# Linear attention and a gated feed-forward layer on one core: the two block transposes of the middle chunks write their 32-word rows side by side, and the plan's numbers are replaced

## The chip, the cores and the metric

The kernel runs on one core of one Trainium2 chip. The time is device time in microseconds (us). Three runs of the kernel before gave 252.01, 252.36 and 253.9 us; the median, 252.36 us, is the time before. A separate execution was taken by the hardware profiler, and all rows shown here come from it.

About 2.5 us either way (1% of the time) is what a measurement of this kernel can tell from no change.

## What is computed

The reference, cut to what matters: a linear attention with products of two 8-wide projections as features, and behind it a feed-forward layer whose gate is a clipped linear function.

```python
batch, n_heads, seq, head_dim, r = 4, 4, 1088, 32, 8
def phi(x):                                   # 64 features per head
    a = einsum('rd,bhsd->bhsr', S1, x)
    b = einsum('rd,bhsd->bhsr', S2, x)
    return einsum('bhsi,bhsj->bhsij', a, b).reshape(..., 64)
kv  = einsum('bhsf,bhsd->bhfd', phi(k), v)
z   = phi(k).sum(axis=2)
x   = einsum('bhsf,bhfd->bhsd', phi(q), kv) / (phi(q) . z + 1e-6)
x   = x.transpose(0, 2, 1, 3).reshape(4352, 128)
h   = x @ w_in                                # 128 x 2048, double precision given
g   = h * clip(h + 3, 0, 6) / 6
out = g @ w_out                               # 2048 x 128
```

## The kernel before

**Chunks.** The 4352 rows are cut into nine chunks of columns (the data lie transposed, a row of x is a column): chunks 0 to 7 have 512 columns, two of each batch, and chunk 8 has the last 64 rows of all four batches, 256 columns. For each chunk the attention gives x (128 x 512), and the feed-forward layer goes over it in eight steps of 256 hidden units.

**A step of the feed-forward layer** (`step`, from L748). x and the weights are split into a high and a low part in a faster float format, so each product is three matmuls: TensorE (PE) makes h (L763, L764, L769, six matmuls for two halves), ScalarE (ACT) makes r = relu(h+3) (L776), VectorE (DVE) makes g = min(r,6)*h (L780), ACT makes the high part gh (L784), GpSimd (POOL) or DVE makes the low part gl = g - gh (L788), and PE adds the products with w_out into o (L807, L808 from gh, L810 from gl). There are two buffers for h, three each for r and g, four each for gh and gl.

**The attention of the keys** (`keys`): PE projects (abps), ACT copies to ab, DVE or POOL multiplies the features ph_k (L458), PE adds up kvps, and the sums of the features over the rows (`total`, L556 to L561) are made by POOL or DVE for batches 1 to 3. ACT copies the result to kvb (L573).

**The attention of the queries.** Chunks 0 and 1 (`queries`) turn their features with PE (phps, L666; copied to phT by ACT, L672), and x again with PE (xps). Chunks 2 to 8 (`far_queries`) turn them with DVE's transpose of 32 x 32 blocks and a trip through device memory: DVE turns ph into pht (L701; L698 for chunk 8), four DMAs write phd (L707), one reads phT (L712), PE makes numerator and denominator (nd, L594), DVE divides (L601 to L605), and for chunks 2 to 7 DVE turns x into xt (L729), four DMAs write xd (L734), one reads xT (L738), ACT makes the high part xh (L635) and DVE or POOL the low part xl (L639). Chunks 2 to 7 are called the middle chunks here. In both of their transposes the result's words are spread out, so that the columns come out in order: neighbouring words of a turned row are written n/2/4 = 64 words apart in L701 and 4 words apart in L729.

**What sets the order.** Every operation is put into a plan with a cost per engine, a due time and the buffers that it needs; `Plan.order` runs a model of the engines over it, takes what is ready in the order of the due times and so fixes the order of instructions on each engine (and for operations marked `dual` whether DVE or POOL does them). The due times come from a table of numbers at the head of the file (L78 to L91): STEP is the planned distance of two steps, LAG the distance from a step's h to its o, LEADS the lead of each attention operation ahead of its chunk's first step. The weights are unpacked from double precision by nine operations per block (L333 to L358, on ACT and DVE), eight blocks in all, during the first 70 us.

The host puts the two parts of the result together (L881 to L883).

Of the kernel before, what the change touches and what calls it, by code (L numbers as in the profile page):

```python
# [80 lines left out]
W_DUE = (23.69, 5.0, 25.05, 37.01, 36.68, 4.34, 28.58, 37.15)
CONV_LEAD = (5.93, -5.53, -0.33, -14.76, 3.75, 22.58, 29.21, 1.33, 1.88)
LOAD_DUE = {'kT_0': -99, 'v_3': -98, 'wiraw0': -97, 'kT_1': -96, 'kT_3': -95, 'qT_1': -94, 'v_0': -93, 'qT_0': -92, 'v_1': -91, 'woraw0': -90, 'v_2': -89, 'kT_2': -88, 'wiraw1': -87}
LEADS = ({'ab': 20.35, 'cp': 18.54, 'ph': 0.97, 'kv': 7.82, 'kvb': 4.29, 'tr': -9.03, 'trcp': 19.03, 'nd': 3.27, 'norm': 21.13, 'xt': 2.41, 'xh': -30.73, 'xl': 17.21, 'k0': 8.88, 'kld': 18.13, 'vld': 11.2, 'qld': -6.47, 'rd': 32.35, 'xw': -22.53, 'xr': -34.19, 'sum': 7.33}, {'ab': 24.06, 'cp': 49.8, 'ph': 14.57, 'kv': 15.67, 'kvb': 12.77, 'tr': -1.26, 'trcp': 2.1, 'nd': 16.83, 'norm': 25.0, 'xt': 46.75, 'xh': 14.66, 'xl': 29.1, 'k0': 3.17, 'kld': 7.72, 'vld': 57.89, 'qld': 71.23, 'rd': 44.5, 'xw': -12.53, 'xr': 8.33, 'sum': -2.02})


HOLD = 5.62
HOLD_DUE = -28.65
SOON = 0.71
SOON_DUE = 11.09  # L90
PATIENCE = 0  # L91

# [193 lines left out]
def fused_kernel(ctx: ExitStack, tc: tile.TileContext, qT, kT, v1, sb, w_in, w_out, outT):  # L286
    nc = tc.nc
# [295 lines left out]
    def divided(c, due, T, t, m, ready, phTb, nb, xb, LEAD, near=True):

# [4 lines left out]
        def nd(_):  # L589
            W["nd"] = bank(nb.tag, f"nd_{c}_{t}")  # L590
            for u, p, e in product(range(m), range(2), (0, HP)):
                o = (2 * u + p) * 2 * DV
# [1 line left out]
                nc.tensor.matmul(W["nd"][e : e + HP, o : o + 2 * DV], T["phT"][:, p, i : i + HP], kvb[batch_of(c0 + i)][:, p, :], start=True, stop=True)  # L594
# [85 lines left out]
    def far_queries(c, due, psb, ndb, ph_eng):  # L680

        LEAD = LEADS[1]
        c0, n = CHUNKS[c]
# [7 lines left out]
        def turn(_):  # L693

            T["turn"] = buf("raw", [P, 4, CH // 2], f"pht_{c}")[:, :, : n // 2]
            src = T["ph"][:, :nt, :].rearrange("p t (e f w) -> p f (t e) w", e=2, w=Q)
            if mixed:
                nc.vector.transpose(T["turn"].rearrange("p f (b w) -> p f b w", w=Q), src)  # L698
# [2 lines left out]
            nc.vector.transpose(out, src.rearrange("p f b (k t) -> p f b k t", t=nt))  # L701

# [22 lines left out]
        def xturn(_):  # L725

            T["xturn"] = buf("xturn", [P, H, nt * Q], f"xt_{c}")
            out = T["xturn"].rearrange("p f (w t) -> p t f w", t=nt)
            nc.vector.transpose(out, T["x"].rearrange("p t (f w) -> p t f w", w=Q))  # L729
# [154 lines left out]
```

## Time and profile before

| | us |
|---|---|
| three runs | 252.01, 252.36, 253.9 |
| the profiled execution, whole | 251.5 |
| its span, first to last instruction | 249.7 |
| transposes pht of chunks 2 to 7 (L701), six | 12.5 |
| transposes xt (L729), six | 6.7 |
| POOL's share of the gl (L788), 41 | 96.6 |
| DVE's share of the gl (L788), 31 | 43.8 |

In the profile a row of the timeline gives start, duration, engine, line, operation, result<-operands, shapes and a count; brackets at its end give the time that the engine stood idle ahead of it and what ended that. PEld is the loading of weights, SPq the queue that issues the DMAs. A matmul's duration covers the filling of its pipeline: matmuls of 512 columns start 0.233 us apart when PE is full (at 104.38, 104.61, 104.84 us and so on), though each is shown with 0.39 us.

### The profile page before, as it was taken

Reading aid. Unit: us, or ns where it says so; the run is one execution under the profiler, and the core shown is the slowest. Engines: PE = TensorE matmul, PEld = TensorE weight load, DVE = VectorE, ACT = ScalarE, POOL = GpSimd, SP = SyncE. Lnnn points to the kernel's source line nnn. Section 1 sums busy time; section 2 is a strip of 40 time slices with the busy share of each in tenths; the row PEclk is TensorE's granted clock in tenths of the full one; section 3 lists DMA queues with packets and bytes.
Section 4 is the critical chain, followed back from the end, with each engine's and each line's share of the span. In section 5 each row is a group of like instructions: output and inputs, shape, how many; then the busy total and the mean of one; then the engine's idle time right before and its main releaser. Section 6 shows DMA issues by size and latency. Waiting matters only on the chain.

```text
span 249.7 us, 4708 instructions
## 1 busy us (share of the span) xinstructions
PE 236.0 (95%) x1816; PEld 183.2 (73%) x1816; DVE 206.8 (83%) x260; ACT 166.5 (67%) x206; POOL 142.5 (57%) x90
## 2 busy tenths in 40 slices
PE   8868999899999899899999998999999999999994
PEld 6656677687677667687887775787878787878894
DVE  1769999999999998786986898988989886467762
ACT  2455698777577666577675765666767776786681
POOL 2515999989589874005835794308750673655302
PEclk9999999999999999999999999999999999999999
DMA  6998833050057156030250313212422130010010
GB/s 209 353 302 306 282 114 84 0 149 23 11 148 190 43 149 204 4 85 0 67 164 3 82 46 86 87 22 62 126 87 43 41 112 18 0 42 0 3 43 21
DMA packets 18006, 23.77 MB, mean 95 GB/s; under 512 B 1728, under 2 KB 11072, under 8 KB 17984
## 3 DMA queue, kind: packets, MB, share of 16 engines
q1 hardware_dynamic: 17984, 23.48, 30.9%
q8 instruction: 14, 0.23, 0.4%
q14 instruction: 8, 0.07, 0.1%
HBM read 16.26 MB, written 7.21 MB: 94 GB/s over the span
## 4 chain that ended last, share of the span: by engine, by line
PE 69%; POOL 11%; DVE 6%; DMA 5%; issue 3%; ACT 2%; SPq 1%; DVEq 0%; ACTq 0%; POOLq 0%
PE o L810 11%; PE o L807 11%; PE o L808 10%; PE h L763 10%; PE h L769 10%; PE h L764 10%; POOL gl L788 7%; PE nd L594 3%; DVE g L780 2%; DMA kT<-kT_dram 2%; POOL ph_q L458 2%; PE abps_k L436 2%; POOL ph_k L458 2%; DMA xT<-xd 1%; DMA xd<-xt 1%
## 5 line engine op out<-in xcount | busy, mean ns | idle before, releaser
L788 POOL TENSOR_TENSOR gl<-g,gh 128x1024 fp32r<-128x1024 f32 (+1 forms) x41 | 96.6, 2360 | 83.9 <-PE o L810 42.3
L776 ACT ACTIVATE r<-h 128x1024 f32<-128x1024 f32 (+1 forms) x72 | 70.4, 979 | 36.6 <-PE h L769 35.0
L780 DVE SCALAR_TENSOR_TENSOR g<-r,h 128x1024 f32<-128x1024 f32 (+1 forms) x72 | 82.2, 1153 | 14.2 <-ACT r L776 8.3
L784 ACT CAST gh<-g 128x1024 fp32r<-128x1024 f32 (+1 forms) x72 | 72.1, 1001 | 21.1 <-PE o L808 13.0
L763 PE MATMUL h<-xh,wi_hi 128*128 128x512 f32 (+1 forms) x144 | 56.5, 392 | 2.8 <-DVE g L780 1.7
L807 PE MATMUL o<-gh,wo_hi 128*128 128x512 f32 (+1 forms) x144 | 55.9, 391 | 0.0
L769 PE MATMUL h<-xl,wi_hi 128*128 128x512 f32 (+1 forms) x144 | 55.0, 383 | 0.0
L764 PE MATMUL h<-xh,wi_lo 128*128 128x512 f32 (+1 forms) x144 | 55.0, 382 | 0.0
L808 PE MATMUL o<-gh,wo_lo 128*128 128x512 f32 (+1 forms) x144 | 54.6, 382 | 0.0
L788 DVE TENSOR_TENSOR gl<-g,gh 128x1024 fp32r<-128x1024 f32 (+1 forms) x31 | 43.8, 1418 | 10.0 <-ACT gh L784 6.0
L810 PE MATMUL o<-gl,wo_hi 128*128 128x512 f32 (+1 forms) x144 | 43.9, 387 | 1.7 <-POOL gl L788 1.7
L763 PEld LDWEIGHTS h<-xh,wi_hi 128*128 128x128 f32 x144 | 27.0, 187 | 10.7 <-PE o L808 1.4
L807 PEld LDWEIGHTS o<-gh,wo_hi 128*128 128x128 f32 x144 | 27.0, 188 | 7.0 <-ACT mag_wo L333 0.4
L810 PEld LDWEIGHTS o<-gl,wo_hi 128*128 128x128 f32 x144 | 25.7, 187 | 8.3 <-POOL gl L788 3.0
L769 PEld LDWEIGHTS h<-xl,wi_hi 128*128 128x128 f32 x144 | 27.0, 188 | 5.8
L808 PEld LDWEIGHTS o<-gh,wo_lo 128*128 128x128 f32 x144 | 27.0, 188 | 5.2
L764 PEld LDWEIGHTS h<-xh,wi_lo 128*128 128x128 f32 x144 | 27.0, 188 | 5.2
L458 POOL TENSOR_TENSOR ph_k<-ab_k 128x512 f32<-128x512 f32 (+1 forms) x9 | 9.1, 1022 | 16.5 <-ACT ab_k L445 16.5
L458 POOL TENSOR_TENSOR ph_q<-ab_q 128x512 f32<-128x512 f32 x14 | 18.2, 1311 | 0.4 <-ACT ab_q L445 0.3
L594 PEld LDWEIGHTS nd<-kvb,phT 128*64 128x64 f32 x272 | 9.1, 137 | 5.1 <-issue 3.0
L701 DVE STREAM_TRANSPOSE pht<-ph_q 128x1024 f32<-128x1024 f32 x6 | 12.5, 2083 | 0.0
L594 PE MATMUL nd<-kvb,phT 128*64 128x66 f32 x272 | 10.9, 226 | 1.1 <-DMA phT<-phd 0.8
(82 smaller groups left out, 185.6 us busy)
## 6 DMA issues: line engine op xcount, KB each, us to landing
phd<-pht SPq DMA_DIRECT2D x24, 128.0 KB, 2.3
phT<-phd SPq DMA_DIRECT2D x6, 512.0 KB, 3.6
wiraw<-w_in_dram SPq DMA_DIRECT2D x4, 512.0 KB, 5.3
qT<-qT_dram SPq DMA_DIRECT2D x8, 256.0 KB, 6.1
woraw<-w_out_dram SPq DMA_DIRECT2D x4, 512.0 KB, 5.1
outT_dram<-os SPq DMA_DIRECT2D x8, 256.0 KB, 2.1
xd<-xt SPq DMA_DIRECT2D x24, 64.0 KB, 1.8
xT<-xd SPq DMA_DIRECT2D x6, 256.0 KB, 2.6
```

The costliest lines, as they stand in the source:

```text
L458: engines[e].tensor_tensor(out, a_, b_, op=ALU.mult)
L594: nc.tensor.matmul(W["nd"][e : e + HP, o : o + 2 * DV], T["phT"][:, p, i : i + HP], kvb[batch_of(c0 + i)][:, p, :], start=True, stop=True)
L763: nc.tensor.matmul(T["h"][:, u, :n], wi_hi[:, f], x, start=True, stop=False)
L764: nc.tensor.matmul(T["h"][:, u, :n], wi_lo[:, f], x, start=False, stop=False)
L769: nc.tensor.matmul(T["h"][:, u, :n], wi_hi[:, f], x, start=False, stop=True)
L776: nc.scalar.activation(T["r"][:, :, :n], T["h"][:, :, :n], AF.Relu, bias=3.0, scale=1.0)
L780: nc.vector.scalar_tensor_tensor(T["g"][:, :, :n], T["r"][:, :, :n], 6.0, T["h"][:, :, :n], op0=ALU.min, op1=ALU.mult)
L784: nc.scalar.copy(T["gh"][:, :, :n], T["g"][:, :, :n])
L788: engines[e].tensor_tensor(T["gl"][:, :, :n], T["g"][:, :, :n], T["gh"][:, :, :n].bitcast(F32), op=ALU.subtract)
L807: nc.tensor.matmul(o, wo_hi[:, f], T["gh"][:, u, :n], start=fp == 0 and u == 0, stop=False)
L808: nc.tensor.matmul(o, wo_lo[:, f], T["gh"][:, u, :n], start=False, stop=False)
L810: nc.tensor.matmul(o, wo_hi[:, f], T["gl"][:, u, :n], start=False, stop=fp == NPAIR - 1 and u == 1)
```

## The change

Both transposes of the middle chunks take the blocks in the order in which they lie in the source and write each block's 32-word rows as neighbouring words. The columns of a middle chunk then come out in another order (four strips of 128 columns are interleaved), which nothing on the chip depends on; the host puts them back. The parameter that told the divisions where the columns lie (`near`) is gone. All numbers of the plan's table are others (of them a line or two is shown), LAG is now a time instead of a multiple of STEP, and some costs in the plan are.

```diff
-LAG = 11.64
+LAG = 25.41
...
-                sums.append(plan.add({POOL: 1.3 * k, DVE: 0.6 * k}, d - LEAD["sum"], [*o3, *sums], total, [phb, sumb], dual=True))
+                sums.append(plan.add({POOL: 1.42 * k, DVE: 0.62 * k}, d - LEAD["sum"], [*o3, *sums], total, [phb, sumb], dual=True))
...
-        kv_done[b] = [plan.add({ACT: 0.23}, due - LEAD["kvb"], [prev], halves, [kvbuf])]
+        kv_done[b] = [plan.add({ACT: 0.43}, due - LEAD["kvb"], [prev], halves, [kvbuf])]
...
-                i = (t + u) * P + e if near else e // HP * n // 2 + (t + u) * HP
+                i = (t + u) * P + e
...
-            src = T["ph"][:, :nt, :].rearrange("p t (e f w) -> p f (t e) w", e=2, w=Q)
-            if mixed:
-                nc.vector.transpose(T["turn"].rearrange("p f (b w) -> p f b w", w=Q), src)
-                return
-            out = T["turn"].rearrange("p f (t b k) -> p f b k t", t=nt, k=Q // nt)
-            nc.vector.transpose(out, src.rearrange("p f b (k t) -> p f b k t", t=nt))
+            src = T["ph"][:, :nt, :].rearrange("p t (e f w) -> p (t e) f w", e=2, w=Q)
+            nc.vector.transpose(T["turn"].rearrange("p f (b w) -> p b f w", w=Q), src)
...
-        a = plan.add({DVE: 0.09 + 0.267 * nt}, due - LEAD["tr"], sorted(set(o3), key=o3.index), turn, [phb, turnb])
+        a = plan.add({DVE: 0.09 + 0.27 * nt}, due - LEAD["tr"], sorted(set(o3), key=o3.index), turn, [phb, turnb])
...
-            out = T["xturn"].rearrange("p f (w t) -> p t f w", t=nt)
+            out = T["xturn"].rearrange("p f (t w) -> p t f w", t=nt)
             nc.vector.transpose(out, T["x"].rearrange("p t (f w) -> p t f w", w=Q))
...
-        a = plan.add({DVE: 0.09 + 0.135 * nt}, due - LEAD["xt"], norms, xturn, [xb, xturnb])
+        a = plan.add({DVE: 0.09 + 0.145 * nt}, due - LEAD["xt"], norms, xturn, [xb, xturnb])
...
-        late = due + LAG * STEP
+        late = due + LAG
...
-    both = {POOL: 0.45, DVE: 0.267}
+    both = {POOL: 0.48, DVE: 0.267}
...
+    far = out[NEAR * CH : B * WHOLE].reshape(-1, P // Q, CH // P, Q, DM).swapaxes(1, 2).reshape(-1, DM)
+    out = np.concatenate([out[: NEAR * CH], far, out[B * WHOLE :]], axis=0)
```

With other numbers in the table the whole order is another. Three places of it. (Behind the line number stand the operation, result<-operands with the buffer's number, and the shape; the lines of the kernel after are 3 lower from the steps on.)

ACT, in the start, where the first batch's kvb is copied. Before:

```order
L445 COPY ab_q_281<-abps_q_258 128x256
L445 COPY ab_q_326<-abps_q_313 128x256
L573 COPY kvb_144<-kvps_272 64x2x33 x2
L333 ACTIVATE mag_wo_384<-woraw_311 128x512
L672 COPY phT_400<-phps_0_374 128x2x2x128
L672 COPY phT_403<-phps_2_386 128x2x2x128
L672 COPY phT_403<-phps_0_393 128x2x2x128
```

After:

```order
L445 COPY ab_k_273<-abps_k_254 128x320
L672 COPY phT_281<-phps_0_268 128x2x2x128
L672 COPY phT_281<-phps_2_276 128x2x2x128
L333 ACTIVATE mag_wi_352<-wiraw_266 128x512
L573 COPY kvb_144<-kvps_286 64x2x33 x2
L445 COPY ab_q_397<-abps_q_374 128x256
```

Two copies of phT and the weight operation (mag) stood behind the copy of kvb and stand ahead of it now.

POOL and DVE, at the sums of the features of batch 2's keys (both halves of the batch: L556, then L558 to L561). Before, on POOL:

```order
L458 TENSOR_TENSOR ph_q_1134<-ab_q_1107 128x512 x2
L556 TENSOR_TENSOR sum_1170<-ph_k_1041 128x512
L788 TENSOR_TENSOR gl_0_1188<-g_0_1138,gh_0_1167 128x1024
L788 TENSOR_TENSOR gl_1_1217<-g_1_1156,gh_1_1186 128x1024
L558 TENSOR_TENSOR sum_1170<-sum_1170,ph_k_1191 128x512
L559 TENSOR_TENSOR sum_1170<-sum_1170,ph_k_1191 128x512
L560 TENSOR_TENSOR sum_1170<-sum_1170,ph_k_1191 128x256
L561 TENSOR_TENSOR sum_1170<-sum_1170 128x256
L788 TENSOR_TENSOR gl_4_1346<-g_4_1287,gh_4_1309 128x1024
```

After, on DVE:

```order
L777 SCALAR_TENSOR_TENSOR g_7_1108<-r_7_1077,h_7_1061 128x1024
L458 TENSOR_TENSOR ph_k_1121<-abps_k_1087,ab_k_1106 128x512 x2
L458 TENSOR_TENSOR ph_k_1121<-abps_k_1087,ab_k_1106 128x256
L558 TENSOR_TENSOR sum_1079<-sum_1079,ph_k_1121 128x512
L559 TENSOR_TENSOR sum_1079<-sum_1079,ph_k_1121 128x512
L560 TENSOR_TENSOR sum_1079<-sum_1079,ph_k_1121 128x256
L561 TENSOR_TENSOR sum_1079<-sum_1079 128x256
L601 TENSOR_SCALAR den_0_1158<-nd_0_1140 128x8
L603 RECIPROCAL rden_0_1160<-den_0_1158 128x8
L605 TENSOR_TENSOR x_1157<-nd_0_1140,rden_0_1160 128x256
L777 SCALAR_TENSOR_TENSOR g_0_1181<-r_0_1165,h_0_1126 128x1024
```

The last four of the five sums went from POOL to DVE, ahead of a division and of the g of chunk 2's first step. The same happens in another place for batch 3's keys, ahead of the g of chunk 4's first step. In all POOL now makes 52 of the 72 gl (41 before), DVE 20 (31 before).

PE, where the low part of one of the two steps 4 of the first two chunks is used (chunks 0 and 1 take turns step by step, so each step stands there twice). Before:

```order
L807 MATMUL o_734<-gh_4_934,wo_hi 128x512
L808 MATMUL o_734<-gh_4_934,wo_lo 128x512
L810 MATMUL o_734<-gl_4_949,wo_hi 128x512 x2
L594 MATMUL nd_2_968<-kvb_146,phT_877 64x66 x8
L763 MATMUL h_6_977<-xh_586,wi_hi 128x512
```

After, just ahead of the same use:

```order
L761 MATMUL h_7_978<-xh_551,wi_lo 128x512
L766 MATMUL h_7_978<-xl_552,wi_hi 128x512
L807 MATMUL o_716<-gl_5_910,wo_hi 128x512 x2
L436 MATMUL abps_k_1004<-s_sb,kT_639 64x64 x8
L804 MATMUL o_774<-gh_4_937,wo_hi 128x512
L805 MATMUL o_774<-gh_4_937,wo_lo 128x512
```

Before, the first h of steps 6 and 7 stand behind the use of gl 4; now they and a projection of keys stand ahead of it (the use itself, of gl_4_947, follows on the four matmuls of gh 4 whose first two are shown), so that more of PE's work lies there between a step's h and the use of its gl.

More of the change, by code (lines that the diff above doesn't have):

```diff
@@ L74 @@
 SPLIT = 2
-STEP = 4.24
-DUES = (-3.53, -2.66, 8.36, 29.13)
-LAG = 11.64
[L81 to L91, printed above, removed]
+STEP = 3.88
+DUES = (-97.17, 16.69, 144.97, 26.48)
+LAG = 25.41
+W_DUE = (213.34, 129.51, -53.04, 57.02, 42.36, 69.04, -12.12, 87.77)
+CONV_LEAD = (-7.3, -110.25, 110.52, -232.21, 32.19, 34.25, 284.17, 95.91, 110.18)
+LOAD_DUE = {'kT_0': -99.0, 'v_3': -88.0, 'wiraw0': -92.0, 'kT_1': -95.0, 'kT_3': -87.0, 'qT_1': -91.0, 'v_0': -94.0, 'qT_0': -97.0, 'v_1': -93.0, 'woraw0': -90.0, 'v_2': -96.0, 'kT_2': -89.0, 'wiraw1': -98.0}
+LEADS = ({'ab': 65.79, 'cp': 87.59, 'ph': -38.82, 'kv': 13.4, 'kvb': 66.99, 'tr': -19.53, 'trcp': -65.04, 'nd': -110.46, 'norm': 130.94, 'xt': 75.73, 'xh': -35.2, 'xl': -82.38, 'k0': -206.76, 'kld': 22.63, 'vld': -5.18, 'qld': -38.58, 'rd': 7.49, 'xw': -123.69, 'xr': -108.27, 'sum': 160.61}, {'ab': 56.41, 'cp': 175.14, 'ph': -71.08, 'kv': 15.48, 'kvb': 8.65, 'tr': 2.52, 'trcp': 40.97, 'nd': 14.31, 'norm': 23.48, 'xt': 1.7, 'xh': -18.86, 'xl': 62.54, 'k0': 13.49, 'kld': -16.71, 'vld': 107.4, 'qld': 67.05, 'rd': 116.53, 'xw': -60.56, 'xr': 105.92, 'sum': 123.01})
+HOLD = 0.11
+HOLD_DUE = 67.05
+SOON = 1.81
+SOON_DUE = 35.22
+PATIENCE = 0.0
 @dataclass(eq=False)
@@ L578, in keys, with divided @@
             prev = plan.add({PE: 0.5}, due - LEAD["kvb"] - 0.5, [a, *sums], turn, [kvbuf, kvTb, sumb], 400)
-        kv_done[b] = [plan.add({ACT: 0.23}, due - LEAD["kvb"], [prev], halves, [kvbuf])]
+        kv_done[b] = [plan.add({ACT: 0.43}, due - LEAD["kvb"], [prev], halves, [kvbuf])]
     x_t, x_ops, x_buf = {}, {}, {}
-    def divided(c, due, T, t, m, ready, phTb, nb, xb, LEAD, near=True):
+    def divided(c, due, T, t, m, ready, phTb, nb, xb, LEAD):
         W = {}
@@ L608, in divided @@
         a = plan.add({PE: 0.03 + 0.3 * m}, due - LEAD["nd"] - lag, [ready, *(o for b in batches for o in kv_done[b])], nd, [phTb, nb, xb], 528 * m)
-        return plan.add({DVE: 0.55 + 0.1 * m}, due - LEAD["norm"] - lag, [a], norm, [nb, xb])
+        return plan.add({DVE: 0.56 + 0.1 * m}, due - LEAD["norm"] - lag, [a], norm, [nb, xb])
     def turn_x(c, due, T, norms, xb, xpb, LEAD):
@@ L718, in far_queries @@
         for t in range(0, nt, 2):
-            norms.append(divided(c, due, T, t, min(2, nt - t), rdop, phTb, Buf(ndb), xb, LEAD, mixed))
+            norms.append(divided(c, due, T, t, min(2, nt - t), rdop, phTb, Buf(ndb), xb, LEAD))
         if mixed:
```

## The prediction

> **What bounds the kernel now.** I read the page first, its busy times and its chain of waits, then the busy times by stage, then PE's timeline for the places where it stands idle.
>
> ```profile
> span 249.7 us, 4708 instructions
> PE 236.0 (95%) x1816; PEld 183.2 (73%) x1816; DVE 206.8 (83%) x260; ACT 166.5 (67%) x206; POOL 142.5 (57%) x90
> PE 69%; POOL 11%; DVE 6%; DMA 5%; issue 3%; ACT 2%; SPq 1%; DVEq 0%; ACTq 0%; POOLq 0%
> ```
>
> PE is busy for 236.0 of 249.7 us and makes 69% of the chain. The change takes nothing from PE's own work, so all that can be won is PE's idle time, 13.7 us, and the time in the start in which it does little. The busy times by stage (bounds; length; PE, PEld, DVE, ACT, POOL; clock; DMA) tell where that idle time lies:
>
> ```profile
> 0.00:24.00 24.00, 19.17 (x389) 15.01 (x389) 15.27 (x38) 10.28 (x21) 8.48 (x18) 1.00 0.89 302
> 24.00:35.00 11.00, 10.38 (x118) 7.15 (x113) 11.00 (x18) 8.02 (x14) 10.54 (x10) 1.00 0.66 228
> 35.00:102.00 67.00, 63.01 (x442) 46.87 (x442) 64.20 (x83) 47.79 (x57) 53.28 (x29) 1.00 0.34 93
> 102.00:200.00 98.00, 96.99 (x622) 75.13 (x619) 85.43 (x90) 67.25 (x75) 48.37 (x26) 1.00 0.23 64
> 200.00:250.00 50.00, 46.47 (x261) 39.01 (x259) 30.87 (x35) 33.14 (x42) 21.88 (x10) 0.99 0.09 30
> ```
>
> In the start PE lacks 4.8 us and is filled up with dummy matmuls besides. From 24 us on DVE is full (11.00 of 11.00, then 64.20 of 67.00), and PE lacks 0.6 and 4.0 us; from 102 to 200 us PE lacks only 1.0 us, and what is left lies in the tail. The waits of PE between 35 and 200 us, from its timeline:
>
> ```profile
> 44.29 0.50 PE L810 MATMUL o<-gl,wo_hi 128*128 128x512 f32 x1 [0.79 <-POOL gl L788]
> 47.69 0.50 PE L810 MATMUL o<-gl,wo_hi 128*128 128x512 f32 x1 [0.33 <-POOL gl L788]
> 63.38 0.50 PE L810 MATMUL o<-gl,wo_hi 128*128 128x512 f32 x1 [0.54 <-POOL gl L788]
> 82.02 0.40 PE L594 MATMUL nd<-kvb,phT 128*64 128x66 f32 x6 [0.77 <-DMA phT<-phd]
> 88.83 0.50 PE L763 MATMUL h<-xh,wi_hi 128*128 128x512 f32 x1 [0.45 <-DVE g L780]
> 101.13 0.50 PE L763 MATMUL h<-xh,wi_hi 128*128 128x512 f32 x1 [1.10 <-ACT xh L635]
> 153.44 0.47 PE L763 MATMUL h<-xh,wi_hi 128*128 128x512 f32 x1 [1.01 <-DVE g L780]
> ```
>
> They add up to 4.99 us, all that PE lacks there. Three are on POOL's gl, two on a g that DVE made late, two on an attention trip through memory that ended late.
>
> **The transposes.** By line, with shapes kept apart (count; busy, mean ns):
>
> ```profile
> L701 DVE STREAM_TRANSPOSE pht<-ph_q 128x1024 f32<-128x1024 f32 x6 | 12.5, 2083 | 0.0
> L729 DVE STREAM_TRANSPOSE xt<-x 128x512 f32<-128x512 f32 x6 | 6.7, 1110 | 0.1
> L698 DVE STREAM_TRANSPOSE pht<-ph_q 128x512 f32<-128x512 f32 x1 | 0.7, 699 | 0.0
> ```
>
> L698, chunk 8's, already writes neighbouring words and takes 699 ns for 512 elements where L729 takes 1110. So xt should fall to 0.70, 0.41 less. For pht with twice the elements 2 x 0.70 = 1.40 is the most; L701 and L729 give (2083 - 1110)/512 = 1.90 ns an element and a fixed part of 0.14, and with that part L698 gives 0.70 + 0.56 = 1.26. I take 1.26, 0.82 less. In all 6 x 0.82 + 6 x 0.41 = 7.4 us of DVE's time. [...]
>
> What of the 7.4 us lies on the path? DVE's rows ahead of the late ones:
>
> ```profile
> 85.66 2.07 DVE L701 STREAM_TRANSPOSE pht<-ph_q 128x1024 f32<-128x1024 f32 x1
> 87.57 1.21 DVE L780 SCALAR_TENSOR_TENSOR g<-r,h 128x1024 f32<-128x1024 f32 x1
> 90.59 1.11 DVE L729 STREAM_TRANSPOSE xt<-x 128x512 f32<-128x512 f32 x1
> 100.46 0.62 ACT L635 CAST xh<-xT 128x512 fp32r<-128x512 f32 x1 [2.03 <-DMA xT<-xd]
> 150.17 2.07 DVE L701 STREAM_TRANSPOSE pht<-ph_q 128x1024 f32<-128x1024 f32 x1
> 152.08 1.21 DVE L780 SCALAR_TENSOR_TENSOR g<-r,h 128x1024 f32<-128x1024 f32 x1
> ```
>
> The g at 87.57, for which PE waits 0.45, stands behind a pht: gone. The xt at 90.59 stands behind the same pht and starts the trip that ends in xh at 100.46, for which PE waits 1.10: 0.82 + 0.41 = 1.23 covers it. The g at 152.08 stands behind a pht: 0.82 of the 1.01. That is 0.45 + 1.10 + 0.82 = -2.4 us. All other transposes lie beside PE's work and are worth nothing by themselves. Bounds: 0, if the order moves these places, and -3.6, if in the stage where DVE is full all its pht and xt count (three and two: 3 x 0.82 + 2 x 0.41 = 3.3) with some of 153.44. A loss I exclude: L698 shows the new form. The wait of 0.77 at 82.02 is for a read of phT behind an earlier pht; the order now has that chunk's transposes ahead by several steps: -0.7 (0 to -0.8).
>
> **The start.** What holds it, from PE, ACT and DVE:
>
> ```profile
> 14.89 0.58 PE L493 MATMUL kvps<-v,ph_k 128*32 128x33 f32 x28 [1.85 <-issue]
> 15.54 0.43 ACT L573 COPY kvb<-kvps 64x66 f32<-64x66 f32 x2 [3.08 <-PE kvps L493]
> 16.00 0.68 ACT L333 ACTIVATE mag_wo<-woraw 128x512 f32<-128x512 f32 x1
> 16.70 1.56 ACT L672 COPY phT<-phps 128x512 f32<-128x512 f32 x3
> 18.08 0.17 DVE L601 TENSOR_SCALAR den<-nd 128x8 f32<-128x8 f32 x1 [2.08 <-PE nd L594]
> ```
>
> DVE stands idle for 2.08 us until the first nd comes, and from there on is full for 50 us; an earlier first nd moves that whole stage. Before, nd had to wait behind kvb (to 15.97), mag (0.68) and the first copy of phT (to about 17.3). Now those copies are done ahead of kvb, and nd can follow it at once: 1.3 us. Besides, the last tile of v that kvps needs is the seventh load of the queue behind the projection's constants instead of the ninth, 2.3 MB down the queue instead of 2.9; at the 302 GB/s of that stage 0.6 MB are 2.0 us. Against that, PE's halt of 1.85 us in kvps is ended by nothing the profile shows and may recur, and the loads ahead of that tile now hold a block of w_in with first place. I take -2.0 (1.3 and a third of the rest; bounds +1.0, half of the 2.0 turned round, and -3.3). Until the first nd DVE's work is about the same.
>
> **The waits for POOL.** The order now lets POOL make more gl (52 x 2.4 us), but gives most of them more time: the use of gl 4 that waited at 63.38 had 6.1 us of matmuls (by 0.233 us each) between its h and itself, and has 13.3 now. Only the first four uses have as little as before (5.4 to 9.3 us; 7.4 to 8.8 before), and it was two of the first five that waited 0.79 and 0.33. I take -1.3 of the 1.66 (bounds 0 and -1.7). Each wait that goes also saves PE's restart (0.50 us in five of the rows above, 0.39 for a matmul in the stream): some five of them, -0.5 (0 to -0.7).
>
> **The sums on DVE.**
>
> ```profile
> L559 POOL TENSOR_TENSOR sum<-sum,ph_k 128x512 f32<-128x512 f32 x3 | 4.8, 1588 | 0.2
> L556 DVE TENSOR_TENSOR sum<-ph_k 128x512 f32<-128x512 f32 x1 | 1.3, 1332 | 0.0
> L458 DVE TENSOR_TENSOR ph_k<-abps_k,ab_k 128x512 f32<-128x512 f32 x8 | 5.2, 685 | 3.0 <-ACT ab_k L445 2.9
> L788 DVE TENSOR_TENSOR gl<-g,gh x31: 692/1226/2710, 77.1 to 244.8; 128x1024 fp32r<-128x1024 f32 x25, 128x512 fp32r<-128x512 f32 x6
> ```
>
> Twice, two additions of 512 and two of 256 go to DVE ahead of a g. The one sum that DVE made took 1.33 us, a product of the same size 0.69; so 1.5 x 0.69 x 2 = 2.1 to 1.5 x 1.33 x 2 = 4.0 us each. The g behind them frees one of two h buffers; PE has another step's h and o to do meanwhile, so I charge half a microsecond each: +1.0 (0 to +8.0, both in full; nearer the low end, because the order puts 3 us and more of o ahead of those h).
>
> **The shorter lag.** The x of chunks 4 and 6 is now asked for late: from the start of nd to the first h that needs xh PE has 11.3 us of work (chunk 4, from its second nd) and 11.2 (chunk 6, from its first). What it took before, from nd on PE to xh:
>
> ```profile
> 134.64 1.16 PE L594 MATMUL nd<-kvb,phT 128*64 128x66 f32 x32
> 146.14 0.61 ACT L635 CAST xh<-xT 128x512 fp32r<-128x512 f32 x1
> 85.63 0.57 PE L594 MATMUL nd<-kvb,phT 128*64 128x66 f32 x12
> 161.62 0.57 PE L594 MATMUL nd<-kvb,phT 128*64 128x66 f32 x12
> 174.12 0.62 ACT L635 CAST xh<-xT 128x512 fp32r<-128x512 f32 x1
> ```
>
> The first pair, 11.5, and 0.6 for xh, less 0.41 for the faster xt, is 11.7: 0.5 late in chunk 6. Behind these places the o of chunk 4's first steps come 5.7 us of matmuls behind their h (20 before): r, g and gh alone need 3.3 us and three hand-overs there, so that nothing is spare. +0.6 (0 to +4.3).
>
> **The sum.** -2.4 - 0.7 - 2.0 - 1.3 - 0.5 + 1.0 + 0.6 = -5.3. The profiled execution took 251.5 us with what lies around its span; that is 0.5 under the lowest of the three runs and 0.9 under their median. 251.5 - 5.3 = 246.2, and 0.5 on it for the runs: 246.7 us.
>
> **The rivals.** *The start and the full stage give all* (chance 0.13): -3.3 in the start, -3.6, -0.8, -1.7, -0.7 and nothing given back: -10.1, 241.9 us. For it: DVE is nearly full from 24 to 102 us, so that each microsecond taken from it there can count. Against: PE has only 4.6 us idle from 24 to 102 us.
>
> *POOL and DVE hold each other up* (0.09): gl on DVE takes 1.23 us at the median and 2.71 at most, so an addition that meets POOL's waits up to 1.5 us. POOL now has 52 gl of 2.4 us and DVE two groups of four sums; if each group waits for one whole gl of POOL, with PE waiting for the g behind, it is 2 x 2.4 more: 251.5, no change. Against: fewer gl on DVE (20) to meet anything. [...]
>
> *The new write pattern is no faster* (0.05), because what slows L701 is something other than its writes: -2.4 and half of the start's gain fall away, 250.1.
>
> *The x of the later chunks comes too late* (0.10; the other side). The trip took 14.83 us once, from 85.63 to 100.46, with other transfers in SP's queue between. With that in chunks 2, 4 and 6, where PE has 12.5, 11.3 and 11.2 us, PE would wait 0.6 + 14.8 - 0.4 less these: 2.5 + 3.7 + 3.8 = 10.0; 246.7 - 0.6 + 10.0 = 256.1. It decides from 8.8 us in all, a trip of some 14.4 us in each of the three. Against it: the longest of the others took 12.5 (161.62 to 174.12).
>
> **How the numbers follow.** The forecast, 244.0 to 249.5 by its own terms, has 0.56; no change for other reasons has 0.07. The range leaves out most of the first rival, the last, and a little beyond: 242.8 to 251.4. A change over 1% is over 2.5 us, about what a measurement of this kernel can tell from none. Faster by that: the forecast and the first rival, 0.69; within it 0.21 (the middle rivals 0.14, the rest 0.07); slower 0.10.
>
> **What would show it.** In the profile after: pht at 1.2 to 1.4 us and xt at 0.7; the first nd less than 0.3 us behind kvb, and before 17; no wait of PE for POOL's gl over 0.3 us behind the first four; PE's waits from 24 to 200 us under 3 us in all; the sums on DVE under 1 us each for 512. I am wrong if pht stays at 2 us, if the first h comes later than 24.05 us as before, or if PE waits for xh or g by over 2 us at the first steps of chunks 2, 4 or 6.

## The result, and the profile after

The changed kernel is slower: 256.39 us (median of 4 runs, 256.27 to 256.64) against 252.44 us for the kernel before (252.01 to 253.9). The ratio is 1.0148, 95% interval 1.0106 to 1.0189. The profiled execution took 256.46 us with a span of 254.7 us; that of before had 249.7. So 5.0 us of span were lost where 5.3 were to be won.

The head of the page after, with the clock's row of the 40 slices:

```profile
span 254.7 us, 4691 instructions
PE 241.4 (95%) x1817; PEld 185.2 (73%) x1817; DVE 189.6 (74%) x251; ACT 165.0 (65%) x206; POOL 163.4 (64%) x99
PEclk9979999999999889999999999999999999999999
PE 83%; DVE 6%; DMA 4%; ACT 3%; issue 2%; SPq 0%; ACTq 0%
```

DVE has 17.2 us less to do than before, and POOL 20.9 more. PE has the same matmuls and is busy for 5.4 us more: it is slower at the same work. By stage (bounds; length; PE, PEld, DVE, ACT, POOL; clock; DMA):

```profile
0.00:24.00 24.00, 19.29 (x354) 15.06 (x354) 14.54 (x34) 10.04 (x21) 9.21 (x19) 0.93 0.82 279
24.00:35.00 11.00, 9.26 (x141) 6.18 (x140) 10.54 (x20) 6.69 (x12) 10.54 (x11) 1.00 0.73 241
35.00:102.00 67.00, 63.37 (x378) 47.52 (x378) 63.31 (x81) 47.45 (x55) 54.35 (x29) 0.97 0.30 86
102.00:200.00 98.00, 98.00 (x669) 73.48 (x668) 67.95 (x84) 62.29 (x72) 61.22 (x30) 1.00 0.27 75
```

From 102 to 200 us PE never stands idle, and from 35 to 102 us it lacks 3.6 us, about as before (4.0). The clock is 0.93 and 0.97 in the first and the third of these stages, where it was 1.00 before. PE's longer waits, from its timeline:

```profile
15.53 0.33 PE L493 MATMUL kvps<-v,ph_k 64*32 64x33 f32 x16 [2.98 <-issue]
34.51 0.48 PE L760 MATMUL h<-xh,wi_hi 128*128 128x512 f32 x1 [1.15 <-DVE g L777]
38.49 0.50 PE L804 MATMUL o<-gh,wo_hi 128*128 128x512 f32 x1 [0.68 <-ACT gh L781]
86.76 0.50 PE L760 MATMUL h<-xh,wi_hi 128*128 128x512 f32 x1 [2.96 <-DVE g L777]
```

None of before's seven waits is there: none for POOL's gl, none for phT, none for xh. In their place stand two of 1.15 and 0.68 in the first steps and one of 2.96 at the first steps of chunk 2. The halt in kvps is 1.1 us longer than before.

DVE's groups with shapes kept apart (count; busy, mean ns): both transposes, and the three sums that went to it.

```profile
L698 DVE STREAM_TRANSPOSE pht<-ph_q 128x1024 f32<-128x1024 f32 x6 | 7.4, 1236 | 0.0
L726 DVE STREAM_TRANSPOSE xt<-x 128x512 f32<-128x512 f32 x6 | 4.2, 708 | 0.1
L558 DVE TENSOR_TENSOR sum<-sum,ph_k 128x512 f32<-128x512 f32 x2 | 2.7, 1350 | 0.0
L559 DVE TENSOR_TENSOR sum<-sum,ph_k 128x512 f32<-128x512 f32 x2 | 4.2, 2106 | 0.1
L560 DVE TENSOR_TENSOR sum<-sum,ph_k 128x256 f32<-128x256 f32 x2 | 2.9, 1454 | 0.1
```

The transposes take 1.24 and 0.71 us, as worked out. The sums do not take what a product of their size takes (0.69). What they met shows in DVE's timeline ahead of the late g, and in POOL's beside it:

```profile
77.21 1.81 DVE L558 TENSOR_TENSOR sum<-sum,ph_k 128x512 f32<-128x512 f32 x1
79.06 2.77 DVE L559 TENSOR_TENSOR sum<-sum,ph_k 128x512 f32<-128x512 f32 x1
81.86 2.48 DVE L560 TENSOR_TENSOR sum<-sum,ph_k 128x256 f32<-128x256 f32 x1
84.38 0.42 DVE L561 TENSOR_TENSOR sum<-sum 128x256 f32<-128x256 f32 x1
85.49 1.21 DVE L777 SCALAR_TENSOR_TENSOR g<-r,h 128x1024 f32<-128x1024 f32 x1
```

```profile
77.18 1.29 POOL L639 TENSOR_TENSOR xl<-xT,xh 128x512 fp32r<-128x512 f32 x1 [0.46 <-ACT xh L635]
78.43 5.63 POOL L785 TENSOR_TENSOR gl<-g,gh 128x1024 fp32r<-128x1024 f32 x2
```

The first sum begins 0.03 us behind POOL's xl and ends 0.55 us behind its end (78.47); the lengths of the second and the third fit a wait for one gl each, and the two gl take 5.63 us where two take 4.85 by their mean of 2.425. In these rows the two engines take turns, instruction by instruction. The four sums take 7.5 us instead of the 2.1 to 4.0 that I had, and the g behind them is late.

The clock in four stretches of 3.41 us, in the columns of the stages (PE's busy time stands first behind the length, the clock third from the end):

```profile
12.77:16.18 3.41, 0.66 (x20) 0.40 (x21) 1.59 (x3) 0.25 (x2) 0.00 (x0) 1.00 1.03 355
16.18:19.59 3.41, 3.41 (x53) 3.10 (x53) 1.31 (x6) 1.60 (x4) 1.85 (x2) 0.50 1.01 344
84.45:87.86 3.41, 1.10 (x5) 0.93 (x6) 3.27 (x9) 1.05 (x1) 0.00 (x0) 1.00 0.00 0
87.86:91.27 3.41, 3.41 (x10) 2.64 (x9) 2.63 (x4) 1.96 (x2) 3.41 (x2) 0.50 0.24 50
```

After each of the two long waits PE runs for 3.41 us at half its clock (0.50), so each of these waits of 3 us costs up to 1.7 us more behind it (half of the 3.41, an estimate). The last place is one without any wait, where kvps is cut into pieces between the matmuls of h:

```profile
114.29 0.40 PE L761 MATMUL h<-xh,wi_lo 128*128 128x512 f32 x1
114.62 0.32 PE L508 MATMUL kvps<-ph_k,v 128*32 128x64 f32 x8
114.87 0.50 PE L766 MATMUL h<-xl,wi_hi 128*128 128x512 f32 x1
115.30 0.32 PE L508 MATMUL kvps<-ph_k,v 128*32 128x64 f32 x8
115.55 0.50 PE L760 MATMUL h<-xh,wi_hi 128*128 128x512 f32 x1
```

An h matmul in the stream comes 0.23 us behind the one before it. From 114.29 to 114.87 pass 0.58 us: 0.23 for that h, and 0.35 for a piece of kvps with four matmuls (8 records); from 114.87 to 115.55 it is 0.45. PE counts as busy throughout, so no view of waits shows what this costs; experiment e5 does.

### The profile page after: what moved, and what is told of

Its sections match the earlier page's. It is cut to its first block, busy times and chain, and to the rows that moved or that the text cites. A ratio compares the mean times of both kernels' runs of the same rounds, so it can differ in the third digit from the quotient of the medians.

```text
span 254.7 us, 4691 instructions
## 1 busy us (share of the span) xinstructions
PE 241.4 (95%) x1817; PEld 185.2 (73%) x1817; DVE 189.6 (74%) x251; ACT 165.0 (65%) x206; POOL 163.4 (64%) x99
## 4 chain that ended last, share of the span: by engine, by line
PE 83%; DVE 6%; DMA 4%; ACT 3%; issue 2%; SPq 0%; ACTq 0%
PE o L807 13%; PE o L804 13%; PE h L760 12%; PE h L766 12%; PE o L805 12%; PE h L761 12%; PE nd L594 3%; DMA qT<-qT_dram 2%; PE abps_k L436 2%; DMA woraw<-w_out_dram 2%; ACT r L773 2%; PE kvps L508 1%; DVE sum L559 1%; PE abps_q L441 1%; DVE sum L560 1%
## 5 line engine op out<-in xcount | busy, mean ns | idle before, releaser
L785 POOL TENSOR_TENSOR gl<-g,gh 128x1024 fp32r<-128x1024 f32 (+1 forms) x52 | 121.2, 2338 | 67.5 <-ACT gh L781 58.0
L766 PE MATMUL h<-xl,wi_hi 128*128 128x512 f32 (+1 forms) x144 | 56.1, 393 | 0.0
L760 PEld LDWEIGHTS h<-xh,wi_hi 128*128 128x128 f32 x144 | 27.3, 189 | 12.3 <-DVE g L777 3.9
L785 DVE TENSOR_TENSOR gl<-g,gh 128x1024 fp32r<-128x1024 f32 (+1 forms) x20 | 27.4, 1375 | 6.8 <-PE o L807 3.4
L458 POOL TENSOR_TENSOR ph_q<-ab_q 128x512 f32<-128x512 f32 x15 | 19.4, 1301 | 6.4 <-ACT ab_q L445 6.4
L458 POOL TENSOR_TENSOR ph_k<-ab_k 128x512 f32<-128x512 f32 (+1 forms) x11 | 10.7, 990 | 9.3 <-ACT ab_k L445 9.2
L594 PEld LDWEIGHTS nd<-kvb,phT 128*64 128x64 f32 x272 | 10.0, 148 | 4.4 <-issue 3.3
L594 PE MATMUL nd<-kvb,phT 128*64 128x66 f32 x272 | 11.9, 237 | 0.1
L316 PE MATMUL warm<-const-bfloat16-1.0 128*128 128x256 bf16 x40 | 8.1, 360 | 0.8 <-PEq L872 0.8
```

The lines of the kernel that those rows point to most:

```text
L458: engines[e].tensor_tensor(out, a_, b_, op=ALU.mult)
L760: nc.tensor.matmul(T["h"][:, u, :n], wi_hi[:, f], x, start=True, stop=False)
L766: nc.tensor.matmul(T["h"][:, u, :n], wi_hi[:, f], x, start=False, stop=True)
L785: engines[e].tensor_tensor(T["gl"][:, :, :n], T["g"][:, :, :n], T["gh"][:, :, :n].bitcast(F32), op=ALU.subtract)
```

## The experiments

All times below are medians beside runs of the kernel before on the same chip (their medians lie between 251.28 and 251.41 us); the ratio is to those. The span is that of the profiled execution. Where a cause is to be placed, I compare the start of one and the same DVE instruction in two traces, which shows to 0.1 us where the two kernels drift apart.

| run | us | ratio to before, 95% interval | span |
|---|---|---|---|
| e1: before's order, new transposes | 249.05 | 0.9903 (0.9863 to 0.9942) | 247.2 |
| e2: after's order, old transposes | 258.48 | 1.0267 (1.0227 to 1.0308) | 257.6 |
| e3: after, sums on POOL | 253.23 | 1.0065 (1.0040 to 1.0091) | 251.7 |
| e4: after, fewer start matmuls | 256.18 | 1.0171 (1.0131 to 1.0212) | 254.6 |
| e5: e3 with kvps gathered | 250.06 | 0.9941 (0.9911 to 0.9972) | 250.0 |
| e6: after, one load later | 255.79 | 1.0158 (1.0106 to 1.0209) | 253.6 |
| e8: after, sums behind three g | 257.61 | 1.0238 (1.0194 to 1.0282) | 255.4 |
| e9: after, two gl on DVE | 253.23 | 1.0069 (1.0042 to 1.0096) | 251.6 |
| e10: e3, e5 and e6 together | 248.96 | 0.9894 (0.9854 to 0.9935) | 247.2 |
| e11: e10 with fewer start matmuls | 249.14 | 0.9880 (0.9831 to 0.9928) | 248.3 |

### e1 and e2: the transposes without the order, and the order without the transposes

e1 is the kernel before with these lines of the change alone (and the reordering on the host):

```diff
-                i = (t + u) * P + e if near else e // HP * n // 2 + (t + u) * HP
+                i = (t + u) * P + e
...
-            src = T["ph"][:, :nt, :].rearrange("p t (e f w) -> p f (t e) w", e=2, w=Q)
...
+            src = T["ph"][:, :nt, :].rearrange("p t (e f w) -> p (t e) f w", e=2, w=Q)
+            nc.vector.transpose(T["turn"].rearrange("p f (b w) -> p b f w", w=Q), src)
...
-            out = T["xturn"].rearrange("p f (w t) -> p t f w", t=nt)
+            out = T["xturn"].rearrange("p f (t w) -> p t f w", t=nt)
```

e2 is the changed kernel with the same lines turned back.

> The kernel before with nothing but the two transposes, the index of the division's reads and the host's reordering of the change; the order of the work is that of before, instruction for instruction. Theory A (the transposes are a gain, and the new order lost it): pht 1.24 us and xt 0.71 as in the changed kernel, and the three waits behind them (0.45 at 88.83, 1.10 at 101.13, 0.82 of 1.01 at 153.44) go: 2.4 us under the kernel before, 249.6 to 250.4. Rival B (the transposes lie beside PE's work everywhere): within 0.6 us of the kernel before. Rival C (the new write pattern itself delays something, such as the writes to memory behind it): slower than before.

> The changed kernel with the two old transposes, the old index of the division's reads and no reordering on the host; the order of the work is that of the changed kernel. Theory A (the order lost the time, and it has taken the transposes off the path in the first chunks): 256.4 to 259, slower than the changed kernel by 0 to 2.4 us, with the wait of about 3 us for g at chunk 2's first step still there. Rival C (the new transposes lost the time): 251 to 253, about the time before.

e1 is faster by 1.0%. The same instructions in the traces of before and of e1 start 0.20 us apart at the first pht (47.62 and 47.42), 0.99 from the xt at 90.59 on (89.60 in e1), 1.72 from the xh at 100.46 on (98.74), and 2.52 from the xt at 165.57 (163.05) to the end. Of these, 0.20 us stood there ahead of the first transpose, so the transposes are worth 2.3 us. PE's h matmuls tell the first step of 0.8 us apart: 0.3 us come at 82.64 (82.16 in e1), where before PE waited for phT, and 0.5 at 88.83 (87.84), where the wait of 0.45 is gone. With 0.7 at 101.13 and 0.8 at 153.44 that is 2.0 us at the three places of the prediction. PE's waits in e1 at the place of the wait for phT and at the last two of the three:

```profile
82.16 0.50 PE L759 MATMUL h<-xh,wi_hi 128*128 128x512 f32 x1 [0.66 <-DVE g L776]
99.41 0.50 PE L759 MATMUL h<-xh,wi_hi 128*128 128x512 f32 x1 [0.38 <-ACT xh L635]
150.92 0.48 PE L759 MATMUL h<-xh,wi_hi 128*128 128x512 f32 x1 [0.22 <-DVE g L776]
```

The first of them is new: where PE waited 0.77 us for phT, it now waits 0.66 for a g, so that little of that wait was won.

e2 is 2.9 us behind the changed kernel by the last instructions they share (its last os at 254.40 for 251.49); 0.6 of that stood there already at the first pht (48.26 for 47.64). So the old transposes cost 2.3 us in the new order too, though not at the same places: 0.8 of it comes with a second unit of half clock at the long wait for g (87.22 to 94.05 us in e2; the changed kernel has half its clock for 3.41 us there). Theory A holds, B and C fall: everything that was lost was lost by the order. Between e1 and the changed kernel, which have the same transposes, lie 7.5 us of span (247.2 and 254.7); the other runs look for those.

### e3: all sums on POOL

```diff
     for op in plan.order():
-        op.emit(op.engine)
+        op.emit(POOL if getattr(op.emit, "__name__", "") == "total" else op.engine)
```

> The changed kernel with all additions of the keys' features on POOL, at the same places of the order (two groups of four go from DVE to POOL). Theory A (the sums on DVE lost most: 2.96 us of wait for the g behind them at 86.76 us, and after it 3.4 us at half the TensorE clock, which is 1.7 us of work): no wait over 0.5 us there, the granted clock 1.00 from 80 to 100 us, and 4.0 to 4.7 us less: 251.7 to 252.6. Rival D (the wait is only moved: POOL's gl are late in place of the g): a wait of PE for POOL's gl or for nd behind the sums, and under 2 us gained, over 254.5. Rival E (the clock falls for another reason than the wait): the wait goes, the slices at 0.5 of the clock stay, 253.4 to 254.

The second and third pht of the trace, the changed kernel first, then e3:

```profile
63.54 1.24 DVE L698 STREAM_TRANSPOSE pht<-ph_q 128x1024 f32<-128x1024 f32 x1
101.15 1.24 DVE L698 STREAM_TRANSPOSE pht<-ph_q 128x1024 f32<-128x1024 f32 x1
```

```profile
64.26 1.24 DVE L698 STREAM_TRANSPOSE pht<-ph_q 128x1024 f32<-128x1024 f32 x1
98.18 1.24 DVE L698 STREAM_TRANSPOSE pht<-ph_q 128x1024 f32<-128x1024 f32 x1
```

From the one to the other the changed kernel takes 37.61 us and e3 33.92: 3.7 us less. The wait for g is 0.61 us in e3, and from 80 to 100 us the clock is 1.00. Behind that nothing changes any more: the two traces stay 2.97 us apart to the end, over batch 3's sums too, so that the second group cost nothing. The end is 3.0 us earlier instead of 3.7 because e3's halt at the start was worse (3.23 us, with the clock at half from 14.0 to 20.9 us, and everything 0.7 us later from there). Theory A is right in its place, and the size is 0.3 us under its lower end; D and E fall.

### e9 and e8: the engine beside it, and the place

e9 gives the two gl that POOL made beside the sums to DVE, behind the sums. e8 leaves the sums on DVE and puts them behind the g of chunk 2's steps 0 to 2.

```diff
+    for o in ops:                                        # e9
+        if o.mark in (("glo", 0, 6), ("glo", 0, 7)):
+            o.engine = DVE
...
+    behind(("sum", 2, 1), ("gate", 2, 2))                # e8
```

> The changed kernel with the two gl that POOL made beside the additions (chunk 0, steps 6 and 7, 78.43 to 84.06 us) given to DVE at the same places of the order, behind the additions. Theory L (an addition on DVE and a gl on POOL shut each other out, instruction by instruction): the additions of batch 2 take 0.69, 0.69, 0.35 and 0.43 us, but for one that meets POOL's xl (1.3 us): 2.2 to 3.5 us together instead of 7.5, though DVE has two gl of 1.2 us more. The wait for g shrinks from 2.96 to under 1.5. Rival M (the additions are slow by their operands): they again take 1.8, 2.8 and 2.5 us.

In e9 the sums take:

```profile
77.58 1.81 DVE L559 TENSOR_TENSOR sum<-sum,ph_k 128x512 f32<-128x512 f32 x1
79.42 0.69 DVE L560 TENSOR_TENSOR sum<-sum,ph_k 128x512 f32<-128x512 f32 x1
80.15 0.43 DVE L561 TENSOR_TENSOR sum<-sum,ph_k 128x256 f32<-128x256 f32 x1
80.61 0.42 DVE L562 TENSOR_TENSOR sum<-sum 128x256 f32<-128x256 f32 x1
```

The first, which meets POOL's xl as before, takes 1.81 again; the others fall from 2.77 and 2.48 to 0.69 and 0.43 us. The operands are the same, the neighbour is gone: theory L. The wait for g falls to 1.00, the clock stays at 1.00, and the end comes 3.1 us earlier although DVE has two gl more. What makes the two engines wait for each other, no run shows.

> The changed kernel with the four additions for batch 2 still on DVE, but behind the g of chunk 2's steps 0 to 2 instead of ahead of them. Theory A (their place ahead of the g cost the time): the wait of 2.96 us at 86.76 goes, the clock stays at 1.00 from 86 to 92 us, 3.0 to 3.8 us less than the changed kernel at the same matmuls, as in e3, where it was 3.7. Rival K (DVE has no room for them in that stretch, wherever they stand): a wait for a later g or for gl takes its place, and under 1.5 us is gained. The additions themselves take 0.7, 0.7, 0.4 and 0.4 us where POOL stands idle beside them, and up to 2.8 where it makes a gl.

In e8 the sums start well and then meet POOL all the same:

```profile
88.21 0.69 DVE L560 TENSOR_TENSOR sum<-sum,ph_k 128x512 f32<-128x512 f32 x1
88.93 0.43 DVE L561 TENSOR_TENSOR sum<-sum,ph_k 128x256 f32<-128x256 f32 x1
89.39 2.48 DVE L562 TENSOR_TENSOR sum<-sum 128x256 f32<-128x256 f32 x1
91.80 2.08 DVE L787 TENSOR_TENSOR gl<-g,gh 128x1024 fp32r<-128x1024 f32 x1
```

The last addition, 256 wide, waits through a gl of POOL (89.13 to 91.59), the gl behind it takes 2.08 us for 1.2, and PE now waits 4.08 us for the g of step 3 at 95.06, with half the clock again behind it (from 94.74 us). So it came out as rival K had it: the wait moved, and nothing was gained (a span of 255.4 us for 254.7). The reason in these rows is not a lack of room on DVE, though, but that an addition and a gl on DVE each met an instruction of POOL again, at another place ahead of a g.

### e5: kvps in one piece

```diff
+    for b in (2, 3):
+        for half in (0, 1):
+            run = [o for o in ops if o.mark == ("kv", b, half)]
+            ops = [o for o in ops if o not in run[:-1]]
+            at = ops.index(run[-1])
+            ops[at:at] = run[:-1]
```

> The kernel of e3 (the changed kernel with all sums on POOL) with one edit more: the kvps matmuls of batches 2 and 3, which stand in PE's order in fifteen pieces of 4 or 8 between matmuls of h, are gathered into four runs (each half of a batch at the place of its last piece). Theory H (each piece costs PE a change of weights that does not hide, 0.20 us ahead of the kvps as at 114.87 and 116.46 us of the changed kernel, and about as much behind it): eleven pieces fewer at 0.2 to 0.4 us, 2.2 to 4.4 us less between 85 and 185 us than e3. Rival I (the pieces cost nothing beyond their matmuls): within 0.5 us of e3.

From the fourth to the seventh pht, first e3 and then e5:

```profile
103.82 1.23 DVE L698 STREAM_TRANSPOSE pht<-ph_q 128x1024 f32<-128x1024 f32 x1
187.69 0.71 DVE L698 STREAM_TRANSPOSE pht<-ph_q 128x512 f32<-128x512 f32 x1
```

```profile
104.98 1.23 DVE L701 STREAM_TRANSPOSE pht<-ph_q 128x1024 f32<-128x1024 f32 x1
185.96 0.71 DVE L701 STREAM_TRANSPOSE pht<-ph_q 128x512 f32<-128x512 f32 x1
```

83.87 us against 80.98: 2.9 us less, and PE waits in neither. Of the eleven pieces fewer, nine lie in this stretch (twelve pieces become three), some 0.32 us each; the other two lie ahead of it and show nothing. The drift sits at the places of the pieces (1.3 us by the last of batch 2's, 1.6 by the last of batch 3's). Theory H, I falls; whether it is the change of weights that costs the time, as theory H says, or something else in the change between the two kinds of matmul, no run separates. The profiled execution shows less (250.0 of span against 251.7) because its halt ended at 16.32, 0.8 us later than e3's, which cost 1.2 us by the first pht; the medians are 3.2 us apart.

### e4, e6 and e11: the halt at the start

PE's matmuls up to the halt are 221 in the trace of before and in that of the changed kernel (second column of the row: matmuls counted), though these are not the same matmuls:

```profile
0.00:14.50 14.50, 11.24 (x221) 8.34 (x222) 8.13 (x19) 4.38 (x9) 5.60 (x15) 1.00 0.84 281
```

```profile
0.00:14.50 14.50, 10.99 (x221) 8.23 (x222) 8.89 (x19) 5.70 (x11) 5.11 (x15) 1.00 0.87 299
```

e4 takes dummy matmuls out ahead of it, e6 takes a load out of the way:

```diff
+    fill_calls = []
+
     def keep_warm(_):
-        ones = nc.const_aps.tensor(1.0, [P, 256], mybir.dt.bfloat16)
-        nc.tensor.matmul(warm[:, :256], ones[:, :P], ones, start=True, stop=True)
+        fill_calls.append(1)                             # e4, e11
+        if len(fill_calls) % 2:
+            ones = nc.const_aps.tensor(1.0, [P, 512], mybir.dt.bfloat16)
+            nc.tensor.matmul(warm[:, :512], ones[:, :P], ones, start=True, stop=True)
...
+    behind(("load", "woraw0"), ("load", "v_3"))          # e6, e10, e11
```

> The changed kernel with every second dummy matmul left out and the others twice as wide (512 columns for 256), so that PE has some 16 fewer matmuls ahead of the halt at 15.53 us. In the kernels before and after the halt stands behind the same matmul of PE's stream, the 221st that the trace counts, though that is another one of the program. Theory F (the halt is PE waiting for its next instructions, and lies at a fixed count): it again comes behind the 221st matmul, which is now behind the last kvps, so that kvb is copied by 13.5 and the first nd comes right behind the halt, at 15.5 to 16.2 instead of 16.98; the halt stays over 2 us long. Rival G (kvps waits for a load of v or for DVE): the halt stays ahead of the last 16 kvps. In time: first nd up to 1.4 us earlier, of which 0 to 1.4 us reach the end, 255.0 to 256.4.

> The changed kernel with one load moved: the first block of w_out (512 KB) goes behind the fourth load of v in SP's order, which is issued at 11.66 us, so that 0.5 MB fewer stand in the DMA queues ahead of PE's instruction packet. [...] Rival J (the packet does not stand behind the loads): the halt ends at 15.4 to 15.8 as before. In time at the end: 0 to 2 us less than the changed kernel, since the load comes later to its first use.

In e4 kvps runs through, and the halt comes behind it, with 220 matmuls counted by then:

```profile
11.65 1.02 PE L497 MATMUL kvps<-v,ph_k 128*32 128x33 f32 x80 [0.25 <-POOL ph_k L462]
16.04 1.12 PE L440 MATMUL abps_q<-s_sb,qT 128*64 128x64 f32 x16 [3.37 <-issue]
```

kvb was copied at 12.74 instead of 15.92, and still the first nd came at 16.95 (16.98 in the changed kernel), since the halt now stood ahead of it. So the halt belongs to a count and not to kvps or its operands. That PE has no instructions there is inferred. In e6 it ends earlier:

```profile
14.12 0.33 PE L496 MATMUL kvps<-v,ph_k 64*32 64x33 f32 x16 [1.67 <-issue]
```

With the load moved it ended at 14.12, 14.20 and 14.30 (e6, e10, e11); in the seven other traces of the new order it ended between 14.94 and 16.32. In all twelve traces one packet of 16 KB of an instruction queue, which I take to be PE's, starts 2.4 to 2.9 us ahead of the halt's end (at 13.0 for 15.53 in the changed kernel, 11.7 for 14.12 in e6, 12.3 for 14.89 before). In e6 the halt ended 1.41 us earlier than in the changed kernel, and 0.5 MB at the 362 GB/s that the changed kernel's queues moved from 12 to 15 us are 1.4 us (an estimate). J falls, then, and theory F as e4 has it, PE waiting for its next instructions, fits. A shorter halt did not keep the clock whole: e6 had half the clock after a halt of only 1.67 us too (0.50 from 14.35 to 17.76; PE had been busy for 1.74 of the 3.41 us ahead), while before's halt of 1.85 us had left the clock whole (1.00 from 13.38 to 16.79). e6 is 1.1 us ahead of the changed kernel by the first pht and keeps that in its trace to the end. Its median does not show it (a ratio of 1.0158, where the changed kernel has 1.0148), so what this edit is worth by itself rests on single traces.

### e10 and e11: the repairs together

> The changed kernel with three repairs together: all sums on POOL (e3), kvps gathered (e5), the first block of w_out behind the fourth load of v (e6). At the same matmuls they gave 3.7, 2.9 and 1.1 us each by themselves. Theory (the three losses are separate): 7.7 us less than the profiled execution of the changed kernel, a span of 247.0, 0.98 to 0.99 of the time before, with the halt in kvps ending at 14.0 to 14.8 and no wait of PE over 1.3 us behind it but the one of 1.3 to 1.9 for g at about 34 us. Rival (with the sums gone from DVE's way the load's place no longer counts, or the halt comes late as in e5): a span of 248.0 to 250.0.

The span is 247.2, as worked out (247.0): against the changed kernel 0.9 us are gained by the first pht (47.64 and 46.76), 4.5 by the fourth, 7.5 at the end. So the three gains add up, as if the losses were separate (0.9 for the start, 3.7 for the sums, 2.9 for kvps), and their sum is as large as the 7.5 us between e1 and the changed kernel. That nothing else in the new order costs or gains time is not shown by that, since other gains and losses can cancel.

> The kernel of e10 with every second dummy matmul left out and the others twice as wide, as in e4, so that PE's halt comes behind the last kvps and kvb is copied by 13. Theory: the halt ends at 14.0 to 14.8 as in e6, the first nd follows within 1.3 us, at 15.0 to 15.9 instead of some 15.6 to 16.6, and the end comes 0 to 1 us earlier than in e10. Rival (something else holds the start: the clock, or DVE that is full from the first nd on): no difference beyond 0.5 us.

In e11 the first nd starts at 14.82 instead of 15.95, and yet the first h at 22.43 instead of 22.46, after a wait of 1.31 us for DVE's xl; then h waits 2.03 us for g at 34.31 and the clock falls to half at 35.35. An nd 1.1 us earlier was worth nothing at the first h. The rival is right: the medians differ by 0.2 us (249.14 and 248.96), and the profiled execution of e11 is 1.1 us longer than e10's.

e1 and e10 are both faster than both kernels of the case, by 1.0% and 1.1% against before; their intervals overlap, so none of the two is shown to be the better.

## Why the prediction was wrong

**The transposes, -2.4 us: right**, in size (1.24 and 0.71 us for 1.26 and 0.70) and in place: e1 gains 2.0 us at the three waits named, and 0.3 more at the wait for phT. The term of -0.7 for that wait counted on the order; with the transposes alone a wait for g took most of its place.

**The sums on DVE, +1.0 us: the step that failed.** It measured 3.7 us (e3), all at the first group. Two things in it were wrong. The additions were priced at 2.1 to 4.0 us a group, from a product of 0.69 us and the one sum of 1.33 us; three of the four of batch 2 met a POOL instruction and waited for it, so that the group took 7.5 us. The row of 1.33 us already showed such a wait, in the trace of before:

```profile
140.00 2.43 POOL L788 TENSOR_TENSOR gl<-g,gh 128x1024 fp32r<-128x1024 f32 x1 [0.98 <-ACT gh L784]
141.64 1.33 DVE L556 TENSOR_TENSOR sum<-ph_k 128x512 f32<-128x512 f32 x1
```

The sum began beside a gl of POOL and ended 0.54 us behind its end, as the first sum of the changed kernel ended 0.55 us behind that of xl. And half a microsecond was charged because PE would have another step's h and o to do; it ran out of them, waited 2.96 us, and then had half its clock for 3.41 us, which was not in the sum at all. A wait of over 2 us for g at the first steps of chunk 2 was one of the signs of being wrong that I had named. The rival in which POOL and DVE hold each other up was what happened (one and the same addition took 2.77 us beside a gl of POOL and 0.69 without, e9); it had 0.09, and counted one gl for a group where three sums met an xl and two gl. The step's bound of +8.0 held what came, but my value was taken at the low end.

**PE's own work: a term that was missing.** I wrote that the change takes nothing from PE's own work, and looked in the order for waits alone. The order cuts kvps of batches 2 and 3 from five runs into fifteen pieces. Gathering them saves 2.9 us from the fourth pht on (e5), and PE counts as busy there with the pieces and without. I gave the pieces no price.

**The start, -2.0 us: not gained.** The first h came 0.55 us earlier (23.50 for 24.05), and by the first pht nothing was left (47.64 for 47.62). I wrote that PE's halt may recur and put that into the bound of +1.0; it recurred behind the same count of matmuls, 1.1 us longer, and held the last kvps. The copy of kvb started at 15.92 instead of 15.54, so that nd, though it followed kvb sooner, came only 0.36 us earlier (16.98 for 17.34), and from 16.18 on PE had half its clock. e11 shows that the step's other assumption was doubtful too: an earlier nd need not move the first h.

**The waits for POOL's gl (-1.3), the restarts (-0.5) and phT (-0.7): the waits went, the time did not come.** PE waits for no gl and no phT in the changed kernel. But 1.15 us for g at 34.51 and 0.68 for gh at 38.49 are new in the same stage; why DVE and ACT are later there I did not separate. Since e10, with three repairs, stands where e1 does (247.2 both), all else that the new order moves comes to about nothing in sum.

**The shorter lag, +0.6: not seen.** PE waited for no xh at chunks 2, 4 and 6, so the rival with the late x did not happen either. It was the only one on the side of slower: slower came, but for other reasons.

The sum over the runs: before to e1 -2.5 (0.2 of it ahead of the first transpose), e1 to the changed kernel +3.7 (sums, with the clock), +2.9 (kvps) and +0.9 (the start, e10's run): +7.5, in all +5.0.

## What to carry to other kernels

An instruction moved to another engine is priced with what runs on its neighbour at that moment, not by its mean: here an addition of 0.69 us took 2.77 beside POOL, and the row that priced it had such a wait in it already. A changed order is read for switches as well as for waits, since PE showed 98.00 of 98.00 us busy while it lost 2.9 us. And a micro-change that comes with a new table should be timed without the table: 1% of gain was hidden under 2.5% of loss.

## What the runs showed of the hardware

In these traces the half clock (0.50) comes in units of 3.41 us on a fixed grid: in the changed kernel it begins at 16.18 and at 87.86, 71.68 us or 21 x 3.413 apart; in e8 at 16.23 and 94.74, which is 23. What brings it on the runs do not settle. Units in which PE was busy for 0.00 (e8), 0.66 and 1.10 (the changed kernel), 1.38 (e11) and 1.74 us (e6) of the 3.41 were followed by one at half the clock. But units with 1.59 (e11, from 11.46), 1.90 (before, from 13.38, by the grid of its last onset at 248.90) and 2.41 us (e9, from 84.69) were not, and a unit of e2 that itself had half the clock, with 2.42 us busy (from 87.22), was followed by another. So a short busy time goes with the half clock, but none of these figures is a threshold. That such a unit does not have to be idle throughout, the 1.10 and 1.74 us show.

PE halts for 1.3 to 3.9 us behind its 221st counted matmul in each of the ten traces with all dummy matmuls in place (the 220th in e4 and e11, where a record may be missing), and goes on 2.4 to 2.9 us after a packet of 16 KB of an instruction queue has started. With the load moved this packet started at 11.68 to 11.83 us (e6, e10, e11), in the seven other traces of the new order at 12.55 to 13.72; that it stands behind loads rests on this edit alone. What sets the 2.4 to 2.9 us from the packet to the end of the halt stays open, and so does a start with so few loads that the halt would vanish, which wasn't tried.
